# A fused retention and feed-forward kernel: the last group's seven products in another order, with PSUM tiles of their own and joined stores

## The chip, the core and the metric

The kernel runs on one core of a Trainium2 chip. A core has TensorE (PE; its weight loads are listed apart as PEld), VectorE (DVE), ScalarE (ACT), GpSimd (POOL) and SyncE (SP), each with its own queue of instructions, executed in order, and 16 DMA engines. Matmuls add into PSUM, which this kernel uses as eight banks of 512 fp32 columns on 128 partitions. The metric is device time in microseconds, the median of several runs.

## The reference

The first half is a linear recurrence per batch and head with a decay per head, the second a feed-forward layer with the activation h + sin(alpha h)^2 / alpha:

```python
for t in range(S):                                  # S = 768, B = 4, H = 8, D = 64
    state = gamma * state + k[:, :, t] (outer) v[:, :, t]
    y[:, :, t] = q[:, :, t] @ state / sqrt(D)
x = y.transpose(0, 2, 1, 3).reshape(B * S, H * D)   # 3072 tokens x 512
h = x @ w_in                                        # 512 -> 2048
s = sin(alpha * h)
g = h + s * s / (alpha + 1e-9)
out = g @ w_out                                     # 2048 -> 512, fp32
```

## The kernel before

The 3072 tokens are 24 tiles of 128, worked in ten groups (4 tiles, eight times 2, and 4). For each group the retention part fills `xT`; then 16 slots follow, one for each block of 128 of the 2048 hidden columns (in the last group). A slot is four matmuls into a PSUM tile `ph` (line 610), a sine and a square on ACT (lines 613 and 618), and one addition on DVE (line 625) that writes a block of `gT`, the transposed g. In the last group, number 9, the slots take the blocks 0, 8, 1, 9, ... 7, 15, so that slots 2m and 2m + 1 make "chunk" m: blocks m and m + 8.

Groups 8 and 9 compute `g @ w_out` with seven block products in place of eight (class `Seven`). For a pair of token tiles the hidden axis is halved (eight blocks each, index j, written `J`) and the 512 output columns are halved (`NH` = 256). Products 3 and 4 have one tile of `gT` on the left and mixed weights `w_mix` on the right; products 5 and 2 have sums of g blocks (`g_mix`, kind "s") and plain `w_out`; products 1, 7 and 6 have sums or differences of both. `g_mix` is made by three additions of line 710 for each chunk, on POOL for chunks 0 to 4 and on DVE for chunks 5, 6 and 7. A product is eight matmuls of 256 columns (line 758). `mm` chooses the accumulator by `IN`: products 5 and 2 go to the two halves of `b`, 4 and 3 to the two halves of `a`, 1 to `c`; later 7 and 6 add onto `a`.

The results leave in four steps. `hold` copies `b` out of PSUM (on ACT, line 767, in the last group). `cross` adds it to `a`, which gives the two off-diagonal output blocks (line 782). `rest` computes `c` minus the held `b` into `t_sb` (line 788). When 7 and 6 have been added, `main` adds `a` and `t_sb` for the two diagonal blocks (line 793). Each block is stored by SP (line 773). All these SBUF tiles (`b_sb`, `o_sb`, `t_sb`) rotate through five buffers, so a new one waits for the store that last read its buffer.

Group 8 is woven between the slots of group 9 (`fast_pieces`). Group 9 is the end of the program (`fast_end`): its first pair of tiles is `x`, its second `y`, and `todo` is the written order of both. For `y` (`split`), products 3 and 6 are done in two halves of 128 columns, so that the last addition and the last store are small: `main(7)`, `main(0)` and `main(1)`. `a` is then `a4` (products 4 and 7) and `a3` (3 and 6), where `a3` is one tile of two banks with a half in each, and `a4` shares the two-bank tile `a4c` with `c`. A tile is handed from writer to reader and back as a whole. PSUM tags are "mm" (four tiles of one bank, also used by the slots' `ph`) and "two" and "pa" (one tile of two banks each).

Where a slot's place carries extra work, `mixes` sets it: `mixes((9, n), f)` runs f behind slot n. The queue of each engine is what this order writes; nothing reorders it later.

Of the kernel before, what the change touches and what calls it, by code (L numbers as in the profile page):

```python
# [8 lines left out]
F32 = mybir.dt.float32  # L9
# [29 lines left out]
def kernel(  # L39
# [15 lines left out]
    nc = tc.nc  # L55
# [5 lines left out]
    d_model = H * D  # L61
# [15 lines left out]
    NG = len(sizes)  # L77
    groups = [order[sum(sizes[:g]):sum(sizes[:g + 1])] for g in range(NG)]
# [5 lines left out]
    psum = ctx.enter_context(tc.tile_pool(name="psum", bufs=1, space=bass.MemoryType.PSUM))  # L84
# [544 lines left out]
    po = {}  # L629
# [24 lines left out]
    FH, NH = FF // 2, d_model // 2  # L654
# [28 lines left out]
    def blocks(t, first, *dims):  # L683

        return bass.AP(t.tensor, t.offset + 128 * first, [t.ap[0]] + [[128 * a, n] for a, n in dims if n > 1] + [[1, 128]])

    def mix_g(g, m, n, eng):

        w = sizes[g]
        if m == 0 and w == 2:  # L690
            for k in ("s0", "s1", "d0", "d1", "x"):
                g_mix[g, k] = big.tile([128, 8 * 128], BF16, name="g_mix", tag="qkr", bufs=10)
        elif m == 0:
            for k in (2, 3):
                g_mix[g, k] = big.tile([128, 5 * 8 * 128], BF16, name="g_mix", tag=f"qk_seq{k}")
        t, h = gT[g], (2, w // 2)
        a, b = m * w, (m + FH) * w
        for op, x0, x1, (to, at), q in (
                (ALU.add, (a, (w, n), (1, w)), (b, (w, n), (1, w)), mixed_g(g, "s", m), w),
                (ALU.subtract, (a + 1, (w, n), h, (b - a - 1, 2)), (a, (w, n), h, (b - a + 1, 2)), mixed_g(g, "d", m), w),  # L700
                (ALU.add, (a, (w, n), h), (b + 1, (w, n), h), mixed_g(g, "x", m), w // 2)):
            i0, i1 = blocks(t, *x0), blocks(t, *x1)
            o = to[:, 128 * at:128 * (at + n * q)]
            if len(i0.ap) == 4:
                o = o.rearrange("p (a b i) -> p a b i", a=i0.ap[1][1], i=128)
            elif len(i0.ap) == 5:
# [3 lines left out]
            eng.tensor_tensor(o, i0, i1, op=op)  # L710

    def mixed_g(g, k, m):

        if sizes[g] == 2:
            return (g_mix[g, "x"], m) if k == "x" else (g_mix[g, f"{k}{m // 4}"], 2 * (m % 4))
        if k == "x":
            return g_mix[g, 2 + m // 4], 32 + 2 * (m % 4)
        return g_mix[g, 2 if k == "s" else 3], 4 * m

    class Seven:  # L720
# [25 lines left out]
        def mm(self, n, j, half=None):  # L746
            k = self.IN[n]
            if self.split and k == "a":
                k = "a4" if n in (4, 7) else "a3"
            t = self.bank(k)  # L750
            r = self.right(n, j)
            if k in ("a", "b"):
                o = t[:, int(n in (2, 3, 6))]
            elif k == "a3":
                o, r, k = t[:, half, 0:128], r[:, 128 * half:128 * half + 128], ("a3", half)
            else:
                o = t
            nc.tensor.matmul(o, self.left(n, j), r, start=k not in self.begun, stop=(j == FH - 1), skip_group_check=True)  # L758
            self.begun.add(k)

        def tmp(self, name):
# [6 lines left out]
            else:  # L768
                by.tensor_copy(self.bsb, self.at["b"])

        def store(self, t, s, n, lo=0, hi=None):
            hi = NH if hi is None else hi
            nc.sync.dma_start(out=out_view[:, groups[self.g][2 * self.p + t], NH * n + lo:NH * n + hi], in_=s)

        def cross(self):
            o = self.tmp("o_sb")
            if self.split:
                nc.vector.tensor_add(o[:, 0], self.at["a4"], self.bsb[:, 1])
                nc.vector.tensor_add(o[:, 1].rearrange("p (x i) -> p x i", x=2), self.at["a3"][:, :, 0:128],
                                     self.bsb[:, 0].rearrange("p (x i) -> p x i", x=2))  # L780
            else:
                nc.vector.tensor_add(o, self.at["a"], self.bsb[:, ::-1])
            self.store(1, o[:, 0], 0)
            self.store(0, o[:, 1], 1)

        def rest(self):
            self.t = self.tmp("t_sb")
# [2 lines left out]
        def main(self, which=None):  # L790
            if which is None:
                o = self.tmp("o_sb")
                nc.vector.tensor_add(o, self.at["a"], self.t)
                self.store(0, o[:, 0], 0)
                self.store(1, o[:, 1], 1)
            elif which == 7:
                self.o = self.tmp("o_sb")
                nc.vector.tensor_add(self.o[:, 0], self.at["a4"], self.t[:, 0])
                self.store(0, self.o[:, 0], 0)
            else:  # L800
                c = slice(128 * which, 128 * which + 128)
                nc.vector.tensor_add(self.o[:, 1, c], self.at["a3"][:, which, 0:128], self.t[:, 1, c])
                self.store(1, self.o[:, 1, c], 1, c.start, c.stop)

        def pieces(self, *parts):
# [293 lines left out]
    def mixes(place, fn):  # L1099
        behind_slot.setdefault(place, []).append(fn)  # L1100
# [14 lines left out]
_INS = ['q', 'k', 'v', 'moe_w_in', 'moe_w_out', 'moe_alpha']  # L1115
# [26 lines left out]
```

## Time and profile before

| | us |
|---|---|
| median of 3 runs | 208.04 |
| lowest and highest run | 207.47, 208.92 |
| the profiled execution | 206.92 |
| its span, first to last instruction | 205.1 |

The profile has one execution. Busy time by engine over the span: PE 195.5 us (95%), PEld 131.4 (64%), DVE 162.3 (79%), ACT 151.7 (74%), POOL 163.4 (80%). Rows of the timeline have the start, the duration from the first to the last end of a merged group, engine, line, operation, tiles and shape, the number of instructions, and in brackets the idle time before it and who ended it. A row that groups by shape has busy time, mean ns of one, then idle time before and its releaser. PE's matmuls overlap, so a gap in issuing is read from start times. POOL and ACT have nothing to do in the last 10 us but ACT's two copies of `b`.

### The profile page before, as it was taken

What the parts mean: (1) busy time and instruction counts of PE and PEld (TensorE: products, weight loads), DVE (VectorE), ACT (ScalarE), POOL (GpSimd) and SP (SyncE); (2) the same over time, 40 slices, a digit from 0 to 9 for tenths busy, and PEclk for the clock granted to TensorE, in tenths of its full rate; (3) what the DMA queues carried; (4) which work ended last, traced back from release to release, by engine and by line L of the source; (5) the groups of instructions that cost most, each with busy time, mean ns of one, the idle gap of its engine ahead of it and who ended that gap; (6) DMA issues with size and microseconds to landing.
All of it is one profiled execution on the core that took longest, in us unless ns stands there. A gap on an engine that the chain in (4) does not pass through costs nothing.

```text
span 205.1 us, 6031 instructions
## 1 busy us (share of the span) xinstructions
PE 195.5 (95%) x2426; PEld 131.4 (64%) x2455; DVE 162.3 (79%) x343; ACT 151.7 (74%) x312; POOL 163.4 (80%) x204
## 2 busy tenths in 40 slices
PE   7889999999999999999999999999999999999992
PEld 7545544457776676676666676766767655556982
DVE  5788599867999988878999796976977965689462
ACT  7779888557997787787687779588686779998020
POOL 8999997999979998797896979998284858994000
PEclk9999999999999999999999999999999999999998
DMA  8999999999999999999992999992714101010133
GB/s 133 153 179 193 200 202 173 167 130 141 235 128 174 96 193 184 185 136 128 212 108 54 156 94 122 116 157 56 107 51 56 54 2 51 3 51 0 54 102 102
DMA packets 103628, 24.82 MB, mean 121 GB/s; under 512 B 93440, under 2 KB 101296, under 8 KB 103600
## 3 DMA queue, kind: packets, MB, share of 16 engines
q0 software_dynamic: 80080, 13.38, 91.2%
q1 hardware_dynamic: 23520, 11.06, 26.5%
q8 instruction: 19, 0.31, 0.6%
q14 instruction: 9, 0.07, 0.1%
HBM read 27.30 MB, written 6.29 MB: 164 GB/s over the span
## 4 chain that ended last, share of the span: by engine, by line
PE 83%; DVE 6%; issue 3%; POOL 2%; DMA 2%; ACT 2%; DVEq 0%; POOLq 0%
PE ph L610 38%; PE po L634 28%; DMA qkr<-in_k_dram 2%; PE a L758 2%; PE ab L758 2%; DVE gT L625 2%; PE py L373 2%; PE b L758 1%; PE a4c L758 1%; POOL qkr L125 1%; PE pt L291 1%; POOL vr L125 1%; PE pa L388 1%; DVE g_mix L710 1%; PE py L446 1%
## 5 line engine op out<-in xcount | busy, mean ns | idle before, releaser
L610 PE MATMUL ph<-xT,w_in 128*128 128x256 bf16 (+3 forms) x653 | 98.0, 290 | 0.3
L625 DVE SCALAR_TENSOR_TENSOR gT<-s,rec_alpha,ph 128x256 bf16<-128x256 f32 (+3 forms) x164 | 79.5, 522 | 22.5 <-ACT s L618 22.0
L613 ACT ACTIVATE s<-ph,alpha_sb 128x256 f32<-128x256 f32 (+3 forms) x164 | 75.8, 505 | 26.6 <-PE ph L610 24.8
L610 PEld LDWEIGHTS <-w_in 128*128 128x128 bf16 x656 | 63.1, 98 | 29.6 <-DVE s_f L568 0.7
L634 PE MATMUL po<-w_out,gT 128*128 128x512 bf16 x264 | 70.3, 379 | 2.3 <-issue 1.9
L618 ACT ACTIVATE s<-s 128x512 f32<-128x512 f32 (+1 forms) x94 | 58.7, 625 | 2.8
L634 PEld LDWEIGHTS <-gT 128*128 128x128 bf16 x288 | 26.4, 98 | 20.9 <-DVE gT L625 0.5
L710 POOL TENSOR_TENSOR g_mix<-gT 128x512 bf16<-128x512 bf16 (+1 forms) x27 | 25.9, 992 | 7.2 <-DVE gT L625 7.2
L149 POOL DMA_DIRECT2D qk_seq<-in_q_dram x32 | 21.6, 719 | 3.1 <-DMA v_seq<-in_v_dram 1.4
L149 POOL DMA_DIRECT2D qk_seq<-in_k_dram x32 | 21.3, 705 | 2.8 <-DMA qk_seq<-in_q_dram 2.8
L149 POOL DMA_DIRECT2D v_seq<-in_v_dram x24 | 16.8, 754 | 0.0
L758 PEld LDWEIGHTS <-g_mix 128*128 128x128 bf16 x128 | 12.0, 98 | 4.6 <-issue 0.9
L681 POOL TENSOR_TENSOR w_mix<-w_out 128x1024 bf16<-128x1024 bf16 x7 | 14.9, 2150 | 0.0
L644 DVE COPY o_sb<-po 128x512 f32<-128x512 f32 x15 | 10.3, 687 | 2.0 <-PE po L634 1.6
L125 POOL DMA_DIRECT2D vr<-in_v_dram x11 | 10.3, 932 | 0.9 <-DMA w_in<-in_moe_w_in_dram 0.7
L189 POOL TENSOR_TENSOR v_seq<-v_seq,kgq 128x512 bf16<-128x512 bf16 x9 | 9.6, 1068 | 1.6 <-DMA v_seq<-in_v_dram 1.6
L407 DVE TENSOR_TENSOR aTw<-pa,maskq 128x768 bf16<-128x768 f32 x10 | 9.5, 954 | 0.2 <-PE pa L421 0.2
L495 DVE TENSOR_TENSOR xT<-py,qg 128x512 bf16<-128x512 f32 x13 | 8.9, 684 | 0.5 <-PE py L453 0.5
L864 PE MATMUL spare<-warm 128*128 128x112 bf16 (+1 forms) x52 | 7.8, 323 | 1.4 <-DVE warm L199 1.2
L391 DVE TENSOR_TENSOR aT<-pa,mask 128x1024 bf16<-128x1024 f32 x7 | 8.5, 1219 | 0.4 <-PE pa L388 0.4
L520 ACT CAST s_q<-s_f 128x256 bf16<-128x256 f32 x13 | 5.1, 395 | 3.4 <-DVE s_f L515 2.7
L125 POOL DMA_DIRECT2D qkr<-in_k_dram x7 | 6.3, 897 | 0.5 <-DMA w_in<-in_moe_w_in_dram 0.5
(141 smaller groups left out, 219.0 us busy)
## 6 DMA issues: line engine op xcount, KB each, us to landing
out_dram<-o_sb SPq DMA_DIRECT2D x18, 256.0 KB, 4.1
w_in<-in_moe_w_in_dram POOLq DMA_DIRECT2D x8, 256.0 KB, 7.9
w_out<-in_moe_w_out_dram POOLq DMA_DIRECT2D x8, 256.0 KB, 7.9
vr<-in_v_dram POOLq DMA_DIRECT2D x11, 128.0 KB, 5.3
out_dram<-o_sb SPq DMA_DIRECT2D x11, 128.0 KB, 1.8
v_seq<-in_v_dram POOLq DMA_DIRECT2D x16, 80.0 KB, 4.5
qkr<-in_q_dram POOLq DMA_DIRECT2D x7, 128.0 KB, 5.9
qkr<-in_k_dram POOLq DMA_DIRECT2D x7, 128.0 KB, 6.2
```

Source lines behind the costliest of these rows:

```text
L125: nc.gpsimd.dma_start(out=t, in_=chunk_of(src, j))
L149: nc.gpsimd.dma_start(out=o, in_=src[bt, head(b, m, e), now[0] * C:(now[-1] + 1) * C, :].rearrange("(f i) d -> i f d", i=64))
L189: eng.tensor_mul(t, t, by[:, j % NCH, :, None].to_broadcast([128, H, D]))
L610: nc.tensor.matmul(self.ph[:, m, :], w_in[:, i, f * 128:(f + 1) * 128], xT[g][:, i, self.lo:self.hi], start=(m == 0 and i == 0), stop=(i = ...
L613: nc.scalar.activation(out=self.s[:, m, :], in_=self.ph[:, m, :], func=ACTF.Sin, scale=alpha_sb[:, f:f + 1])
L618: nc.scalar.activation(out=self.s, in_=self.s, func=ACTF.Square)
L625: nc.vector.scalar_tensor_tensor(gT[self.g][:, f, self.lo:self.hi], self.s[:, m, :], rec_alpha[:, f:f + 1], self.ph[:, m, :], op0=ALU.mult ...
L634: nc.tensor.matmul(po[g, ts], gT[g][:, f, ts * C:(ts + 1) * C], w_out[:, f, :], start=(f == 0), stop=(f == FF - 1))
L644: nc.vector.tensor_copy(o_sb, po[g, ts])
L681: eng.tensor_tensor(w_mix[n, i], w_block(*a, js), w_block(*b, js), op=op)
L710: eng.tensor_tensor(o, i0, i1, op=op)
L758: nc.tensor.matmul(o, self.left(n, j), r, start=k not in self.begun, stop=(j == FH - 1), skip_group_check=True)
```

## The change

Four things change, all in the last two groups; what is computed stays.

1. `fast_end`: the first seven chunks of products 3 and 4 and the first five of 5 and 2 are done for x, then the same for y; then the last three chunks of 5 and 2, `hold`, and the eighth chunk of 3 and 4, then `cross`, for x and for y. After that x's products 1, 7, 6 with `rest` and `main` are wholly ahead of y's.
2. PSUM: x's `b` and `c` use the "pa" tag one after the other; y's `a3` becomes two tiles `a30` and `a31` of the "mm" tag, `a4` has the "two" tile alone, and y's `c` is an "mm" tile.
3. `cross` and `main` of the last group store both blocks in one transfer (`store_both`). So that one access pattern serves, the halves of `a` swap places: `main` now reads `a` reversed where `cross` read `b_sb` reversed.
4. On DVE the mix of chunk 5 moves from behind slot 12 to behind slot 14, and that of chunk 6 from behind slot 14 to behind slot 15.

```diff
         def mm(self, n, j, half=None):
...
-                k = "a4" if n in (4, 7) else "a3"
+                k = "a4" if n in (4, 7) else f"a3{half}"
             t = self.bank(k)
             r = self.right(n, j)
             if k in ("a", "b"):
-                o = t[:, int(n in (2, 3, 6))]
-            elif k == "a3":
-                o, r, k = t[:, half, 0:128], r[:, 128 * half:128 * half + 128], ("a3", half)
-            else:
-                o = t
+                t = t[:, int(n in (2, 4, 7))]
+            elif half is not None:
+                r = r[:, 128 * half:128 * half + 128]
...
+        def store_both(self, o, n):
+
+            t0, t1 = groups[self.g][2 * self.p:2 * self.p + 2]
+            if self.g < NG - 1:
+                self.store(0, o[:, 0], n)
+                self.store(1, o[:, 1], 1 - n)
+                return
+            to = bass.AP(out.tensor, out.offset + t0 * 128 * d_model + NH * n,
+                         [[d_model, 128], [(t1 - t0) * 128 * d_model + (NH if n == 0 else -NH), 2], [1, NH]])
+            nc.sync.dma_start(out=to, in_=o)
 
         def cross(self):
             o = self.tmp("o_sb")
             if self.split:
-                nc.vector.tensor_add(o[:, 0], self.at["a4"], self.bsb[:, 1])
-                nc.vector.tensor_add(o[:, 1].rearrange("p (x i) -> p x i", x=2), self.at["a3"][:, :, 0:128],
-                                     self.bsb[:, 0].rearrange("p (x i) -> p x i", x=2))
+                nc.vector.tensor_add(o[:, 1], self.at["a4"], self.bsb[:, 1])
+                for h in range(2):
+                    c = slice(128 * h, 128 * h + 128)
+                    nc.vector.tensor_add(o[:, 0, c], self.at[f"a3{h}"], self.bsb[:, 0, c])
             else:
-                nc.vector.tensor_add(o, self.at["a"], self.bsb[:, ::-1])
-            self.store(1, o[:, 0], 0)
-            self.store(0, o[:, 1], 1)
+                nc.vector.tensor_add(o, self.at["a"], self.bsb)
+            self.store_both(o, 1)
...
-                nc.vector.tensor_add(o, self.at["a"], self.t)
-                self.store(0, o[:, 0], 0)
-                self.store(1, o[:, 1], 1)
+                nc.vector.tensor_add(o, self.at["a"][:, ::-1], self.t)
+                self.store_both(o, 0)
...
     def fast_end(g):
-        J, J0, J1, J2 = range(FH), range(FH - 1), range(FH - 1, FH), range(FH - 3, FH)
-        J5 = range(FH - 3)
+        J, J0, J1 = range(FH), range(FH - 1), range(FH - 1, FH)
+        K0, K1 = range(FH - 3), range(FH - 3, FH)
 
         def near_banks(k):
-            if k == "c":
-                return psum.tile([128, NH], F32, name="c", tag="mm", bufs=4)
+            if k in ("b", "c"):
+                return psum.tile([128, 2, 512], F32, name=k, tag="pa")[:, 0].rearrange("p (x n) -> p x n", x=2)[:, slice(0, 2) if k == "b" else 0]
             return psum.tile([128, 2, NH], F32, name=k, tag="mm", bufs=4)
 
         def far_banks(k):
             if k == "b":
-                return near_banks(k)
-            if k == "a3":
-                return psum.tile([128, 2, 512], F32, name="a3", tag="pa")
-            if "a4c" not in po:
-                po["a4c"] = psum.tile([128, 2, 512], F32, name="a4c", tag="two")
-            return po["a4c"][:, int(k == "c"), 0:NH]
+                return psum.tile([128, 2, NH], F32, name=k, tag="mm", bufs=4)
+            if k == "a4":
+                return psum.tile([128, 2, 512], F32, name=k, tag="two")[:, 0, 0:NH]
+            return psum.tile([128, NH if k == "c" else 128], F32, name=k, tag="mm", bufs=4)
         x, y = Seven(g, 0, near_banks), Seven(g, 1, far_banks, True)
-        todo = x.pieces((3, J), (4, J0)) + y.pieces((3, J), (4, J0)) + x.pieces((5, J5), (2, J5)) + y.pieces((5, J5), (2, J5))
-        todo += x.pieces((4, J1)) + y.pieces((4, J1)) + x.pieces((5, J2), (2, J2), x.hold, x.cross)
-        todo += y.pieces((5, J2), (2, J2), y.hold, y.cross) + x.pieces((1, J), x.rest) + y.pieces((1, J), y.rest)
-        todo += x.pieces((7, J), (6, J), x.main)
-        todo += y.pieces((7, J), lambda: y.main(7), (6, J, 0), lambda: y.main(0), (6, J, 1), lambda: y.main(1))
+        todo = x.pieces((3, J0), (4, J0), (5, K0), (2, K0)) + y.pieces((3, J0), (4, J0), (5, K0), (2, K0))
+        todo += x.pieces((5, K1), (2, K1), x.hold, (3, J1), (4, J1), x.cross)
+        todo += y.pieces((5, K1), (2, K1), y.hold, (3, J1), (4, J1), y.cross)
+        todo += x.pieces((1, J), x.rest, (7, J), (6, J), x.main)
+        todo += y.pieces((1, J), y.rest, (7, J), lambda: y.main(7), (6, J, 0), lambda: y.main(0), (6, J, 1), lambda: y.main(1))
...
-        mixes((9, 2 * m + 1 + (m in (5, 6))), lambda m=m: mix_g(9, m, 1, nc.gpsimd if m < 5 else nc.vector))
+        mixes((9, 2 * m + 1 if m < 5 else min(15, m + 9)), lambda m=m: mix_g(9, m, 1, nc.gpsimd if m < 5 else nc.vector))
```

The change moves instructions on three engines. First DVE at the end of group 9's slots, before: the rows of line 625 are the additions of slots 12, 13, 14 and 15, those of line 710 the mixes of chunks 5 and 6 (three each), and line 793 is the last addition of group 8.

```order
L625 SCALAR_TENSOR_TENSOR gT_3495<-s_3674,rec_alpha_138,ph_3673 128x512
L710 TENSOR_TENSOR g_mix_3522<-gT_3495 128x512
L710 TENSOR_TENSOR g_mix_3523<-gT_3495 128x512
L710 TENSOR_TENSOR g_mix_3523<-gT_3495 128x256
L625 SCALAR_TENSOR_TENSOR gT_3495<-s_3689,rec_alpha_138,ph_3688 128x512
L625 SCALAR_TENSOR_TENSOR gT_3495<-s_3702,rec_alpha_138,ph_3701 128x512
L710 TENSOR_TENSOR g_mix_3522<-gT_3495 128x512
L710 TENSOR_TENSOR g_mix_3523<-gT_3495 128x512
L710 TENSOR_TENSOR g_mix_3523<-gT_3495 128x256
L793 TENSOR_TENSOR o_sb_3728<-ab_3504,t_sb_3668 128x512
L625 SCALAR_TENSOR_TENSOR gT_3495<-s_3717,rec_alpha_138,ph_3716 128x512
```

The same place now:

```order
L625 SCALAR_TENSOR_TENSOR gT_3495<-s_3674,rec_alpha_138,ph_3673 128x512
L625 SCALAR_TENSOR_TENSOR gT_3495<-s_3686,rec_alpha_138,ph_3685 128x512
L625 SCALAR_TENSOR_TENSOR gT_3495<-s_3699,rec_alpha_138,ph_3698 128x512
L710 TENSOR_TENSOR g_mix_3522<-gT_3495 128x512
L710 TENSOR_TENSOR g_mix_3523<-gT_3495 128x512
L710 TENSOR_TENSOR g_mix_3523<-gT_3495 128x256
L801 TENSOR_TENSOR o_sb_3725<-ab_3504,t_sb_3668 128x512
L625 SCALAR_TENSOR_TENSOR gT_3495<-s_3714,rec_alpha_138,ph_3713 128x512
```

The additions of slots 13 and 14 passed the mix of chunk 5, and the mix of chunk 6 went behind slot 15's addition, ahead of chunk 7's.

Second PE, at the start of the first product into `c`. Before, x's product 1 ends there and y's begins, with its wait for DVE:

```order
L758 LDWEIGHTS g_mix_3523 [waits DVE_49]
L758 MATMUL c_3826<-w_mix_2596,g_mix_3523 128x256
L758 LDWEIGHTS g_mix_3522
L758 MATMUL a4c_3769<-w_mix_2383,g_mix_3522 128x256 [waits DVE_49]
L758 LDWEIGHTS g_mix_3522
```

Now, y's eighth chunk of products 3 (two halves) and 4, then x's product 1:

```order
L756 LDWEIGHTS gT_3495
L756 MATMUL a30_3762<-w_mix_2381,gT_3495 128x128
L756 LDWEIGHTS gT_3495
L756 MATMUL a31_3770<-w_mix_2381,gT_3495 128x128
L756 LDWEIGHTS gT_3495
L756 MATMUL a4_3778<-w_mix_2333,gT_3495 128x256
L756 LDWEIGHTS g_mix_3522
L756 MATMUL c_3826<-w_mix_2383,g_mix_3522 128x256 [waits Activation_49]
```

The wait of `c` moved from y's to x's product and from DVE's additions to ACT's copy of x's `b`.

Third PE again, where y's product 6 goes from its first half of the columns to its second, before:

```order
L758 LDWEIGHTS g_mix_3523
L758 MATMUL a3_3752<-w_mix_2895,g_mix_3523 128x128
L758 LDWEIGHTS g_mix_3523
L758 MATMUL a3_3752<-w_mix_2895,g_mix_3523 128x128 [waits DVE_49]
L758 LDWEIGHTS g_mix_3523
```

and now:

```order
L756 LDWEIGHTS g_mix_3523
L756 MATMUL a30_3762<-w_mix_2895,g_mix_3523 128x128
L756 LDWEIGHTS g_mix_3523
L756 MATMUL a31_3770<-w_mix_2895,g_mix_3523 128x128 [waits DVE_49]
L756 LDWEIGHTS g_mix_3523
```

Both wait for a count of DVE's instructions. Before it was that of `main(0)`, the addition that reads the first half just written; now it is that of y's `cross`, which last read the tile `a31`.

More of the change, by code (lines that the diff above doesn't have):

```diff
@@ L752, in mm @@
             if k in ("a", "b"):
-                o = t[:, int(n in (2, 3, 6))]
-            elif k == "a3":
-                o, r, k = t[:, half, 0:128], r[:, 128 * half:128 * half + 128], ("a3", half)
-            else:
-                o = t
-            nc.tensor.matmul(o, self.left(n, j), r, start=k not in self.begun, stop=(j == FH - 1), skip_group_check=True)
+                t = t[:, int(n in (2, 4, 7))]
+            elif half is not None:
+                r = r[:, 128 * half:128 * half + 128]
+            nc.tensor.matmul(t, self.left(n, j), r, start=k not in self.begun, stop=(j == FH - 1), skip_group_check=True)
             self.begun.add(k)
@@ L769, in hold, with store @@
                 by.tensor_copy(self.bsb, self.at["b"])
-        def store(self, t, s, n, lo=0, hi=None):
-            hi = NH if hi is None else hi
+        def store(self, t, s, n, lo=0, hi=NH):
             nc.sync.dma_start(out=out_view[:, groups[self.g][2 * self.p + t], NH * n + lo:NH * n + hi], in_=s)
+        def store_both(self, o, n):
[7 more added lines that the diff above has]
+            nc.sync.dma_start(out=to, in_=o)
         def cross(self):
@@ L801, in main @@
                 c = slice(128 * which, 128 * which + 128)
-                nc.vector.tensor_add(self.o[:, 1, c], self.at["a3"][:, which, 0:128], self.t[:, 1, c])
+                nc.vector.tensor_add(self.o[:, 1, c], self.at[f"a3{which}"], self.t[:, 1, c])
                 self.store(1, self.o[:, 1, c], 1, c.start, c.stop)
```

## Prediction

> **What bounds the kernel now.** I read the page first, then the chain that ended last, then the timeline of the last 17 us engine by engine, then the waits and the output stores. TensorE (PE) is busy for 95% of the span, and the change touches only what happens after the last feed-forward slot, from about 188 us on. So the question is how much of those last 17 us is not PE work. The chain of waits there, in order of time (start us, us, what):
>
> ```profile
> 188.53 0.67 DVE gT L625
> 189.20 0.05 issue
> 189.25 1.94 PE a L758 x24
> ...
> 195.04 0.59 ACT b_sb L767
> 195.64 0.02 issue
> 195.66 0.69 DVE o_sb L782
> 196.35 0.40 DVE o_sb L778
> 196.75 0.04 issue
> 196.79 1.03 PE a4c L758 x8
> ...
> 200.93 0.30 DVE o_sb L802
> 201.24 0.04 issue
> 201.28 0.62 PE a L758 x8
> 201.90 0.02 issue
> 201.92 0.29 DVE o_sb L802
> ```
>
> Three times the chain leaves PE for VectorE (DVE) and comes back: at 189.25 PE waited for an addition that makes gT, at 196.79 for the addition of line 778, at 201.28 for the addition of line 802. To price these I need the pace at which PE issues when nothing holds it. The timeline of PE has the groups ahead of each wait, and the groups by shape have the length of one matmul:
>
> ```profile
> 187.98 0.93 PE L758 MATMUL a<-w_mix,gT 128*128 128x256 bf16 x7
> 195.50 1.04 PE L758 MATMUL c<-w_mix,g_mix 128*128 128x256 bf16 x8
> 200.28 0.61 PE L758 MATMUL a<-w_mix,g_mix 128*128 128x128 bf16 x8
> ...
> L758 PE MATMUL c<-w_mix,g_mix 128*128 128x256 bf16 x8 | 1.0, 272 | 0.0
> L758 PE MATMUL a<-w_mix,g_mix 128*128 128x128 bf16 x16 | 1.2, 219 | 0.4 <-DVE o_sb L802 0.4
> ```
>
> Eight matmuls of 256 columns in 1.04 with the last one 0.27 long are (1.04 - 0.27)/7 = 0.110 us apart; eight of 128 columns are (0.61 - 0.22)/7 = 0.056 apart. So the eighth `a` was due at 187.98 + 7 x 0.110 = 188.75 and came at 189.25: **0.50** lost. The first `a4c` was due at 195.50 + 8 x 0.110 = 196.38 and came at 196.79: **0.41**. The second half of `a3` was due at 200.28 + 8 x 0.056 = 200.73 and came at 201.28: **0.55**. Together 1.46 us. Everything else from 187.98 on is PE issuing back to back.
>
> **The change part by part.** The amount of PE work stays: the same 128 matmuls (40 + 56 of 256 columns, 32 of 128) are issued in another order. Where PE starts also stays, because ScalarE (ACT) paces the slots before it and none of its instructions moves. These are ACT, GpSimd (POOL) and DVE near that place, and the busy time in the stretch 184 to 188 us (PE, PEld, DVE, ACT, POOL, clock, DMA):
>
> ```profile
> 184.00:188.00 4.00, 4.00 (x28) 2.44 (x26) 3.66 (x7) 3.90 (x8) 3.05 (x4) 1.00 0.07 25
> ...
> 187.27 0.63 ACT L618 ACTIVATE s<-s 128x512 f32<-128x512 f32 x1
> 188.51 0.63 ACT L618 ACTIVATE s<-s 128x512 f32<-128x512 f32 x1
> ...
> 184.15 2.90 POOL L710 TENSOR_TENSOR g_mix<-gT 128x512 bf16<-128x512 bf16 x3
> ...
> 186.11 1.76 DVE L710 TENSOR_TENSOR g_mix<-gT 128x512 bf16<-128x512 bf16 x3
> 187.80 1.39 DVE L625 SCALAR_TENSOR_TENSOR gT<-s,rec_alpha,ph 128x512 bf16<-128x512 f32 x2
> 189.11 0.95 DVE L710 TENSOR_TENSOR g_mix<-gT 128x512 bf16<-128x512 bf16 x3
> 189.99 0.68 DVE L793 TENSOR_TENSOR o_sb<-ab,t_sb 128x512 f32<-128x512 f32 x1
> 190.59 0.73 DVE L625 SCALAR_TENSOR_TENSOR gT<-s,rec_alpha,ph 128x512 bf16<-128x512 f32 x1
> ```
>
> ACT is busy 3.90 of 4.00 us and ends the squares of slots 14 and 15 at 187.90 and 189.14.
>
> *Eighth chunks last, mixes moved on DVE.* The wait at 189.25 is for chunk 7, which slot 14's addition writes; its square ended at 187.90, but DVE was in the mix of chunk 5, which took 1.76 because POOL mixed until 187.05 (the next mix took 0.95). Now that mix stands behind slot 14's addition. My DVE times: slot 14's addition 187.92 to 188.65, mix 5 to 189.60, the last output addition of group 8 to 190.28, slot 15's addition to 191.01, mixes 6 and 7 to 192.92. PE's times at 0.110 and 0.056: x's 14 of products 3 and 4 to 189.52, its 10 of products 5 and 2 to 190.62, y's 14 half-width to 191.40 and 7 wide to 192.17, its 10 to 193.27. Nothing waits: the accumulator `a4` needs group 8's addition (190.28, reached at 191.40), y's `b` needs slot 15's buffer (191.01, reached 192.17), the last chunks of products 5 and 2 need mix 7 (192.92, reached 193.27), chunk 7 of products 3 and 4 is reached only at 193.9. Saved: 0.50. The tightest cover is mix 7's, 0.35 us; its first instruction alone is what products 5 and 2 read, so the true cover is larger.
>
> *Own accumulators.* y's product 1 (`c`) no longer lies in one tile with `a4`, so its 0.41 goes. In its place x's `c` takes over the tile of x's `b` and so waits for the ACT copy of line 767, and x's product 7 waits for x's cross addition. ACT and DVE take:
>
> ```profile
> L767 ACT COPY b_sb<-b 128x512 f32<-128x512 f32 x2 | 1.2, 585 | 6.0 <-PE b L758 5.9
> L782 DVE TENSOR_TENSOR o_sb<-a,b_sb 128x512 f32<-128x512 f32 x1 | 0.7, 692 | 3.3 <-ACT b_sb L767 3.3
> L793 DVE TENSOR_TENSOR o_sb<-a,t_sb 128x512 f32<-128x512 f32 x1 | 0.7, 692 | 1.1 <-PE a L758 1.1
> L802 DVE TENSOR_TENSOR o_sb<-a,t_sb 128x128 f32<-128x128 f32 x2 | 0.6, 292 | 0.7 <-PE a L758 0.7
> L778 DVE TENSOR_TENSOR o_sb<-a4c,b_sb 128x256 f32<-128x256 f32 x1 | 0.4, 425 | 0.0
> L779 DVE TENSOR_TENSOR o_sb<-a,b_sb 128x256 f32<-128x256 f32 x1 | 0.4, 415 | 0.0
> ```
>
> x's last `b` is issued by 193.93 and ends 0.16 later; the copy runs 194.11 to 194.70. PE meanwhile issues two matmuls of x, y's six and three of y, to 195.04: the copy is covered by 0.34 us. x's cross addition ends at 195.41, product 7 is reached at 195.92: cover 0.51. The new waits cost 0.
>
> *The two halves of product 6 apart.* `a3` becomes two tiles, so the second half no longer waits for the reading of the first: 0.55 saved. No row shows PE writing one half while DVE reads the other, so the price lies between 0 and the whole 0.55; the nearest row is PE issuing 128-column matmuls at 0.056 from 200.28 while DVE read `a4c` from 200.49, undisturbed, and I take 0. The Trainium skill, PSUM — Partial Sum Buffer, section on bank collisions, has engines kept apart by bank (and quadrant of partitions); the halves already lay in two banks, so by it the old wait came from the tile alone and all 0.55 goes; a hold in the chip itself would leave 0.91 of the 1.46. The undisturbed row agrees with the page.
> y's cross now adds the halves in two instructions: 2 x 0.292 - 0.415 = 0.17 more on DVE. They end near 196.6, and x's last addition is due only at 197.8: covered, 0. If DVE were late, x's product outputs would be, not PE.
>
> *Stores.* From x's cross on SyncE issues 6 transfers where it issued 9. Its issues and their landings, and two stretches (engines as above, then the clock, the DMA engines' share and GB/s):
>
> ```profile
> L773 SPq DMA_DIRECT2D out_dram<-o_sb x13: 332/399/424, 182.6 to 202.2; - x13
> DMA to landing us min/median/max: 1.7/1.8/1.8
> ...
> DMA to landing us min/median/max: 2.0/3.1/6.7
> ...
> 194.00:196.00 2.00, 2.00 (x21) 1.80 (x19) 0.34 (x1) 0.89 (x2) 0.00 (x0) 1.00 0.00 0
> 201.50:202.00 0.50, 0.38 (x7) 0.21 (x4) 0.08 (x1) 0.00 (x0) 0.00 (x0) 1.00 0.81 273
> ```
>
> The first landing row is of these stores, the second of line 647's, 256 KB each in the middle of the kernel. An issue costs SyncE 0.33 to 0.42. Fewer issues earlier save nothing, since the last store (64 KB, split as before) still follows the last addition; the price of the joined form is unknown, between the 1.8 of 128 KB and the 6.7 of a 256 KB store. I take 1.8 plus 128 KB more at the 273 GB/s of the last row, 0.5: 2.3 us. Who needs it: y's `t_sb` reuses the buffer of x's cross and waits for its store (issued about 195.45, landed 197.75, needed 198.72 when y's `c` is done), and x's joined store waits for the same landing on SyncE, with y's last three stores queued behind it. Cover 0.97: cost 0. Group 8's swap of which operand is read backwards is 0 too: line 782 with a reversed operand takes 0.692, line 793 without one 0.692 as well.
>
> **Sum.** -0.50 - 0.41 - 0.55 = -1.46. PE's last matmul moves from 201.90 to 200.44 (the paces added up from 187.98 give 200.50), the last addition from 202.21 to 200.75; what follows it (2.89 us to the end of the span) stays. The profiled execution took 206.92 for a span of 205.1; it would become 205.46. That execution lies 1.12 under the median of the runs, 208.04, so the forecast on the median is 208.04 - 1.46 = **206.6 us**, 0.7% faster. About 1% is what a measurement of this kernel can tell from no change.
>
> **The rivals.**
> *A new wait takes the old ones' place.* If x's ACT copy or its cross addition comes over 0.3 to 0.5 us later than I put it, PE stands before `c` or `a` again. The old hand-overs cost 0.41 and 0.55; two such back leave 1.46 - 0.96 = 0.50: 207.5. For it: the covers of 0.34 to 0.51 are small. Against it: in the old chain the copy began 0.02 after its releaser and took its 0.59.
> *The end is not PE's.* If the stores' own stream set the end, an earlier PE would bring nothing: 208.0. For it: in 201.5 to 202.0 the DMA engines are 81% busy. Against it: the last store landed in the shortest time of all, 1.7, and now the same bytes are spread over a longer stretch.
> *The joined store lands late (slower).* It has 198.72 - 195.45 = 3.27 us. From 3.27 + 1.46 = 4.7 on the kernel is slower than before; at the 6.7 of the longest 256 KB store it is 6.7 - 3.27 = 3.43 later than my forecast: 210.0. Against it: those stores ran beside loads, and here the DMA share is 0.00 in 194 to 196; their median of 3.1 would still just do. [...]
>
> **How the numbers follow.** Forecast 0.66, a new wait 0.17, the end not PE's 0.11, the late store 0.06. Runs of the kernel before lie within 1.45 of each other, half of which, 0.73, I allow on the forecast: 205.85 to 207.3. The range reaches up to the new wait's 207.5 with 0.3 of that allowance, 207.8, and down to 205.5 by half of it more, since the median shown may itself stand high beside its profile. It leaves out the last two rivals, 0.17. Faster by over 1% means under 205.96, a quarter of the forecast's case: 0.17. Slower by over 1% means above 210.1, half of the late store and a little noise: 0.04. Within 1%: 0.79.
>
> **What would show it.** Right: no PE gap of 0.3 us or more between 188 and the last matmul, which comes about 12.4 us after the first `a`; mix 5 at 0.95; PE's waits for the additions of the old lines 778 and 802 gone; y's `t_sb` not waiting for a DMA. Wrong: PE waiting for ACT before x's `c`, for DVE before x's product 7 or before the last chunks of products 5 and 2, joined stores over 3.3 us to landing, or a later first `a`.

## The result, and the profile after

| us | before | after |
|---|---|---|
| median of 20 runs each | 207.75 | 206.38 |
| ratio to before, 95% interval | | 0.9937, 0.9913 to 0.9962 |
| the profiled execution, its span | 206.92, 205.1 | 207.02, 205.2 |
| first matmul into x's `a` | 187.98 | 189.66 |
| end of the last DVE addition | 202.21 | 202.41 |
| the stretch between the two | 14.23 | 12.75 |
| the tail, from there to the end of the span | 2.89 | 2.79 |

The kernel is 0.63% faster, with the interval 1.31 us, 0.79 to 1.81: inside the forecast's range, and within 1%, as forecast. One of the 20 executions of before took 407.21 us; without it their median is 207.68. The one profiled execution of the kernel after does not show it in its span, which is 0.1 longer. It reached the first matmul into x's `a` 1.68 us later than the execution of before, and up to there the two programs do the same work but for one moved mix; the distance stood already long before, while data was still loaded (SP issued one and the same store of line 647 at 74.17 before and at 75.99 after). So the two are compared from that matmul on: 1.48 us less in the stretch and 0.10 less in the tail. Spans are printed to a tenth of a microsecond here, so a tail is good to 0.05; in the trace the two spans are 205.125 and 205.227, and the tails 2.91 and 2.81.

The chain of waits after, in order of time (start us, us, what):

```profile
189.38 0.44 PE ab L756 x4
189.82 1.53 PE a L756 x14
191.35 1.09 PE b L756 x10
192.44 1.55 PE a L756 x21
193.99 1.75 PE b L756 x16
...
196.82 0.87 PE c L756 x8
197.70 1.75 PE a L756 x16
199.44 0.87 PE c L756 x8
200.32 1.78 PE a L756 x24
202.10 0.02 issue
202.12 0.29 DVE o_sb L809
```

In the chain of before DVE stood three times between two stretches of PE. Now the chain stays on PE from the last slots to the last matmul, and only the last addition follows. The busy time by engine over the stretch says the same. First of the kernel after, then of the kernel before (PE, PEld, DVE, ACT, POOL, clock, DMA share, GB/s):

```profile
189.60:202.20 12.60, 12.48 (x131) 11.21 (x128) 8.91 (x22) 2.35 (x4) 0.00 (x0) 1.00 0.24 85
```

```profile
187.90:202.30 14.40, 13.00 (x131) 11.19 (x128) 8.78 (x19) 2.38 (x5) 0.00 (x0) 1.00 0.23 77
```

PE is idle for 0.12 of 12.60 us, where it was idle for 1.40 of 14.40. The view of PE's waits in this part of the program has three rows before, and none after:

```profile
PE a L758 <- DVE o_sb L802: 0.4, 1, 0.4
PE a L758 <- DVE gT L625: 0.3, 1, 0.3
PE a4c L758 <- DVE o_sb L778: 0.3, 1, 0.3
```

How near the new hand-overs are is read from the timeline after:

```profile
192.40 1.83 DVE L710 TENSOR_TENSOR g_mix<-gT 128x512 bf16<-128x512 bf16 x6
193.82 1.91 PE L756 MATMUL b<-w_out,g_mix 128*128 128x256 bf16 x16
...
195.77 0.58 ACT L765 COPY b_sb<-b 128x512 f32<-128x512 f32 x1 [4.95 <-PE b L756]
...
196.38 0.69 DVE L791 TENSOR_TENSOR o_sb<-a,b_sb 128x512 f32<-128x512 f32 x1 [2.15 <-ACT b_sb L765]
...
196.66 1.04 PE L756 MATMUL c<-w_mix,g_mix 128*128 128x256 bf16 x8
...
197.53 1.91 PE L756 MATMUL a<-w_mix,g_mix 128*128 128x256 bf16 x16
```

x's copy of `b` ends at 196.35 and x's `c` takes over the tile at 196.66: 0.31 to spare. x's cross addition ends at 197.07 and product 7 starts at 197.53: 0.46. The mixes of chunks 6 and 7 end at 194.23; the last chunks of products 5 and 2 are the last six of the group at 193.82, reached ten matmuls of 0.110 later, at 194.92: 0.69.

### The profile page after: what moved, and what is told of

It reads as the page before. It is cut to its first block, busy times and chain, and to the rows that moved or that the text cites. A ratio compares the mean times of both kernels' runs of the same rounds, so it can differ in the third digit from the quotient of the medians.

```text
span 205.2 us, 6029 instructions
## 1 busy us (share of the span) xinstructions
PE 195.2 (95%) x2426; PEld 131.4 (64%) x2455; DVE 161.5 (79%) x344; ACT 151.8 (74%) x312; POOL 163.2 (80%) x204
## 4 chain that ended last, share of the span: by engine, by line
PE 83%; DMA 7%; POOL 4%; issue 2%; DVE 2%; ACT 1%; POOLq 0%
PE ph L610 37%; PE po L634 28%; DMA qkT<-qkr 4%; PE a L756 3%; DMA qkr<-in_q_dram 3%; PE ab L756 3%; POOL qkr L125 2%; PE b L756 2%; PE py L373 1%; POOL vr L125 1%; PE c L756 1%; PE pt L291 1%; PE pa L388 1%; PE py L437 1%; POOL w_in L161 1%
## 5 line engine op out<-in xcount | busy, mean ns | idle before, releaser
L165 POOL DMA_DIRECT2D w_out<-in_moe_w_out_dram x8 | 5.8, 727 | 1.2 <-DMA w_in<-in_moe_w_in_dram 0.8
```

## The experiments

The theory: three stalls of PE were the whole difference, each is removed by one part of the change, and the stores bring nothing. The rivals: a part does nothing here, or removes another part's stall too; the new hand-overs are nearly late; the end is set by something other than PE. Since the time up to the first `a` differs from one execution to the next, each kernel is judged by the stretch and the tail as defined above:

| | first `a` | last addition's end | stretch | span | tail |
|---|---|---|---|---|---|
| before | 187.98 | 202.21 | 14.23 | 205.1 | 2.89 |
| after | 189.66 | 202.41 | 12.75 | 205.2 | 2.79 |
| before, with the mixes moved | 195.78 | 209.50 | 13.72 | 212.4 | 2.90 |
| after, mixes in the old places | 189.92 | 202.68 | 12.76 | 205.5 | 2.82 |
| after, `c` beside `a4` | 188.37 | 202.07 | 13.70 | 204.9 | 2.83 |
| after, `a3` one tile | 188.48 | 201.78 | 13.30 | 204.4 | 2.62 |
| after, stores apart | 188.17 | 200.93 | 12.76 | 204.0 | 3.07 |
| after, x's copy twice | 188.17 | 201.28 | 13.11 | 204.1 | 2.82 |
| after, old order of products 1, 7, 6 | 196.25 | 209.00 | 12.75 | 211.9 | 2.90 |
| after, five matmuls fewer | 188.42 | 200.63 | 12.21 | 203.5 | 2.87 |

**The mixes alone.** The kernel before, with only the fourth part of the change.

```diff
-        mixes((9, 2 * m + 1 + (m in (5, 6))), lambda m=m: mix_g(9, m, 1, nc.gpsimd if m < 5 else nc.vector))
+        mixes((9, 2 * m + 1 if m < 5 else min(15, m + 9)), lambda m=m: mix_g(9, m, 1, nc.gpsimd if m < 5 else nc.vector))
```

> The kernel before with only the mixes of chunks 5 and 6 moved on DVE (part 4 of the change). I measure the end stretch: from the first matmul into x's a to the end of the last addition; it is 14.23 us in the kernel before and 12.75 in the changed one. My theory, that the first of the three stalls is slot 14's addition standing behind the 1.76 us mix: that addition now ends near 0.7 us after the first a, the stall of 0.50 goes or shrinks under 0.1, the other two (0.41 and 0.55) stay, the stretch is 13.75. Rival, that only the later place of chunk 7 in PE's order removes it: the stretch stays at 14.2.

The stretch is 13.72, 0.51 under that of before. Of the three waits of PE two are left:

```profile
PE a L758 <- DVE o_sb L802: 0.4, 1, 0.4
PE a4c L758 <- DVE o_sb L778: 0.3, 1, 0.3
```

So the wait for chunk 7 goes by the moved mix alone. Its time as a whole, 214.18, has nothing to do with the end: 7 us were lost from 104 us on (see the last section).

**The mixes back.** The kernel after, with that line as it was before (the diff above the other way round).

> The changed kernel with the mixes of chunks 5 and 6 where they were. Theory: PE reaches chunk 7 of products 3 and 4 only about 6 us after its first a, and mix 7 keeps over 0.3 us of cover, so nothing waits: stretch 12.75. Rival, that moving the mixes carries the first stall's 0.50: 13.25.

The stretch is 12.76, no longer. The mix of chunk 5 took 1.76 us again, between slot 12's and slot 14's additions, and no one waits for it, since chunk 7 is now first read at 195.84, 4.7 us behind slot 14's addition. So the 0.50 is removed by the late eighth chunk or by the moved mix, by either alone; with the new order the fourth part of the change has no share in the time.

**`c` beside `a4`.** The kernel after, with y's `c` and `a4` in one tile of two banks as before.

```diff
-            if k == "a4":
-                return psum.tile([128, 2, 512], F32, name=k, tag="two")[:, 0, 0:NH]
-            return psum.tile([128, NH if k == "c" else 128], F32, name=k, tag="mm", bufs=4)
+            if k in ("a4", "c"):
+                if "a4c" not in po:
+                    po["a4c"] = psum.tile([128, 2, 512], F32, name="a4c", tag="two")
+                return po["a4c"][:, int(k == "c"), 0:NH]
+            return psum.tile([128, 128], F32, name=k, tag="mm", bufs=4)
```

> The changed kernel with y's c again in the second bank of the tile that holds y's a4. Theory: y's product 7 now comes right behind product 1, so with one tile it must wait until t_sb has read c (c's last matmul ends 0.16 after product 7 could start, the subtraction takes 0.69): a PE stall of 0.9, stretch 13.65. Rival, that the old stall of 0.41 came from the order of the products alone: 12.75; or it comes back as it was: 13.15.

The stretch is 13.70, and PE's row before y's product 7 has the reason:

```profile
197.99 1.04 PE L756 MATMUL a4c<-w_mix,g_mix 128*128 128x256 bf16 x8
199.81 1.03 PE L756 MATMUL a4c<-w_mix,g_mix 128*128 128x256 bf16 x8 [0.78 <-DVE t_sb L796]
```

Product 1 ends, DVE reads `c` into `t_sb`, and only then product 7 may write `a4` in the same tile. In the order of before x's products 7 and 6 stood between them. So the shared tile costs 0.95 in the new order, more than the 0.41 that it cost in the old one: the order with x wholly ahead can be had only with the tile of its own.

**`a3` as one tile.** The kernel after, with the two halves in two banks of one tile, and `a4` in a one-bank tile.

```diff
-            if k == "a4":
-                return psum.tile([128, 2, 512], F32, name=k, tag="two")[:, 0, 0:NH]
-            return psum.tile([128, NH if k == "c" else 128], F32, name=k, tag="mm", bufs=4)
+            if k[:2] == "a3":
+                if "a3" not in po:
+                    po["a3"] = psum.tile([128, 2, 512], F32, name="a3", tag="two")
+                return po["a3"][:, int(k[2]), 0:128]
+            return psum.tile([128, NH], F32, name=k, tag="mm", bufs=4)
```

> The changed kernel with y's a30 and a31 again as the two banks of one tile (a4 in a tile of its own instead). Theory: the second half of product 6 waits for the addition that reads the first, 0.55 comes back, stretch 13.30. Rival, that the new order hides it: 12.75.

The stretch is 13.30: the whole 0.55 is back, at the old place.

```profile
200.85 0.61 PE L756 MATMUL a<-w_mix,g_mix 128*128 128x128 bf16 x8 [0.38 <-DVE o_sb L809]
```

The banks of the halves are two in both kernels; only the tile differs. With two tiles PE writes one half while DVE reads the other, and nothing is held: the 24 matmuls from 200.16 in the kernel after follow each other at the pace of before. The Trainium skill, PSUM — Partial Sum Buffer, section on bank collisions, lets two engines work on different banks at once; the runs agree, with 0.55 against 0.

**Stores apart.** The kernel after, with nine stores again in place of six.

```diff
-            if self.g < NG - 1:
+            if self.g < NG:
```

> The changed kernel with the joined stores of the last group as two stores each again. Theory: the stores are off the path, stretch 12.75 and the tail from the end of the last addition to the end of the span 2.8 as now, within 0.1. Rival, that fewer stores shorten the tail (it is 2.79 now, 2.89 in the kernel before): the tail is 2.9 or more.

The stretch is the same, 12.76, and the tail is 3.07, the rival's side: the stores were not worth nothing. What differs is looked at in the runs on the tail below.

**x's copy twice.** The kernel after, with ACT's copy of x's `b` made two times, one after the other.

```diff
-                nc.scalar.copy(self.bsb, self.at["b"])
+                for _ in range(2 - self.p):
+                    nc.scalar.copy(self.bsb, self.at["b"])
```

> The changed kernel with x's b copied twice by ACT, so that the copy that c waits for ends 0.6 us later. It measures the cover of the new wait, 0.31 by the trace of the changed kernel. Theory: PE stands 0.6 - 0.3 = 0.3 before x's c, x's product 7 keeps waiting for nothing, stretch 13.05. Rival, a new wait that already sets the pace: the whole 0.6, stretch 13.35. If the copy were of no account: 12.75.

The stretch grew by 0.36, to 13.11, where the copy had grown by 0.59:

```profile
195.53 1.03 PE L756 MATMUL c<-w_mix,g_mix 128*128 128x256 bf16 x8 [0.20 <-ACT b_sb L766]
```

So the copy has some 0.23 to spare up to the point at which PE's issue is really late (0.59 - 0.36), a little less than the 0.31 between its end and `c`, of which the hand-over takes part. The tightest of the new waits is this one.

**The old order of the last products.** The kernel after, with products 1, 7 and 6 in the order of before, on the new tiles.

```diff
-        todo += x.pieces((1, J), x.rest, (7, J), (6, J), x.main)
-        todo += y.pieces((1, J), y.rest, (7, J), lambda: y.main(7), (6, J, 0), lambda: y.main(0), (6, J, 1), lambda: y.main(1))
+        todo += x.pieces((1, J), x.rest) + y.pieces((1, J), y.rest) + x.pieces((7, J), (6, J), x.main)
+        todo += y.pieces((7, J), lambda: y.main(7), (6, J, 0), lambda: y.main(0), (6, J, 1), lambda: y.main(1))
```

> The changed kernel with x's product 1 and y's product 1 in a row again, then x's 7 and 6, then y's 7 and 6 (the first pair no longer wholly ahead), with the new tiles. Theory: with c in a tile of its own the order of the products brings nothing to PE, stretch 12.75; x's last store of 256 KB leaves 0.9 us later and meets the last three, so the tail may grow from 2.79 to 2.9. Rival, that having the first pair ahead carries the 0.41: 13.15.

The stretch is 12.75. Once `c` has its own tile, having x wholly ahead brings nothing. (This execution also lost 7 us from 104 us on, see the last section.)

**Five matmuls fewer.** The kernel after, without the first five matmuls of x's product 2.

```diff
-        todo = x.pieces((3, J0), (4, J0), (5, K0), (2, K0)) + y.pieces((3, J0), (4, J0), (5, K0), (2, K0))
+        todo = x.pieces((3, J0), (4, J0), (5, K0)) + y.pieces((3, J0), (4, J0), (5, K0), (2, K0))
```

> The changed kernel without the first five matmuls of x's product 2, whose part of the sum is left out. Theory, that PE's issuing sets the end: 5 x 0.11 = 0.55 less, stretch 12.2, unless mix 7, which had about 0.7 of cover, is met: down to 12.2 all the same. Rival, that DVE or the stores set the end: 12.75 or a tail longer by 0.5.

The stretch is 12.21, 0.54 less: five times 0.110. What PE issues still comes out at the end in full, so the end is PE's, and the stores do not set it.

**The tail.** The tail has two pieces: from the end of the last addition to SP's issue of the last store, and from there to the end of the span. SP's stores at the end, their issue and landing, by line; the last number before the semicolon is when the last one was issued. Before, after, and with the stores apart:

```profile
L773 SPq DMA_DIRECT2D out_dram<-o_sb x9: 332/399/424, 196.4 to 202.2; - x9
```

```profile
L770 SPq DMA_DIRECT2D out_dram<-o_sb x3: 345/384/393, 201.7 to 202.6; - x3
...
DMA to landing us min/median/max: 1.6/1.7/1.8
```

```profile
L770 SPq DMA_DIRECT2D out_dram<-o_sb x9: 332/382/443, 195.6 to 201.1; - x9
...
DMA to landing us min/median/max: 1.7/1.7/1.8
```

By the timeline the last issue was at 202.24 before, 0.03 after its addition; at 202.60 after, 0.19 behind it; at 201.10 with the stores apart, 0.17 behind it. So the kernel after lost 0.16 here: its last two additions start 0.44 apart (201.68 and 202.12), where before the stall of 0.55 had set them 0.99 apart, and an issue of 0.35 to 0.39, with the wait ahead of it, does not fit in between any more. With the stall back (`a3` as one tile) the last store is issued at 201.81, 0.03 behind its addition again, and the tail is 2.62, the shortest of the first eight runs. From the last issue to the end it is 2.86 before and 2.90 with nine stores, 2.60 after with six, though the last store lands in 1.6 to 1.7 in all of them. Two runs went after the two pieces.

One store on ACT's queue: the small store of `main(0)` is issued by ACT, which has nothing else to do there.

```diff
-        def store(self, t, s, n, lo=0, hi=NH):
-            nc.sync.dma_start(out=out_view[:, groups[self.g][2 * self.p + t], NH * n + lo:NH * n + hi], in_=s)
+        def store(self, t, s, n, lo=0, hi=NH, by=nc.sync):
+            by.dma_start(out=out_view[:, groups[self.g][2 * self.p + t], NH * n + lo:NH * n + hi], in_=s)
...
-                self.store(1, self.o[:, 1, c], 1, c.start, c.stop)
+                self.store(1, self.o[:, 1, c], 1, c.start, c.stop, nc.sync if which else nc.scalar)
```

> The kernel after, with one store, that of the last token tile's first half of its main block, issued from ACT's queue instead of SP's, so that SP issues only one store in the last 0.6 us. In the kernel after, SP was still issuing the store before until 202.50, and issued the last one at 202.60, 0.19 us after the addition's end at 202.41. Theory (SP's issuing delays the last store, and the tail carries the delay): the stretch from the first matmul into x's a to the last addition's end stays 12.75 us, the last store is issued 0.03 to 0.05 us after the addition, and the tail falls from 2.79 to about 2.63 us, so the whole is 0.15 us below the kernel after, 1.46 us below before. Rival (what follows the last landing takes the gain back, or ACT's queue is later at it): the tail stays at 2.75 us or more.

The first `a` is at 188.43, the last addition ends at 201.18, the span is 203.8: a stretch of 12.75 and a tail of 2.62, and SP issued its last store 0.03 after the addition, in the timeline:

```profile
200.77 0.37 ACTq L770 DMA_DIRECT2D out_dram<-o_sb  x1
...
201.21 0.34 SPq L770 DMA_DIRECT2D out_dram<-o_sb  x1
```

Its median is 205.51, and the ratio to before 0.9888 (0.9856 to 0.9921). This is 0.87 under the median of the kernel after, far more than the 0.17 of the tail, so both were timed side by side on one chip, as they are. The kernel after:

> The kernel after as it stands, timed beside the version with one store on ACT's queue, on one chip. The single profiles give that version 0.17 us less behind the last addition (2.62 against 2.79 us) and the same stretch before it, 12.75 us. Theory (the store's queue is all that differs, the rest of the distance between the two medians, 206.38 and 205.51 us, is spread from the loading phase): the two medians here lie 0.1 to 0.5 us apart. Rival (moving that store also changes what comes before): they lie 0.8 us or more apart, as they did.

And the one with a store on ACT's queue:

> The version with one store on ACT's queue, beside the kernel after on the same chip. Theory: its median is 0.1 to 0.5 us under that kernel's, and the tail of its profile is 2.6 us again, with a stretch of 12.75 us. Rival: 0.8 us or more under it; or no difference at all, with a tail of 2.75 us or more.

The medians are 205.93 and 205.66, 0.27 apart; the stretches 12.76 and 12.75; the tails 2.78 (204.4 - 201.62) and 2.65 (203.9 - 201.25). By the unrounded spans of the traces the tail is shorter by 0.17 in the first pair of executions and by 0.18 in the second, so this part is repeatable. Their ratios to before, 0.9902 (0.9867 to 0.9936) and 0.9909 (0.9878 to 0.9940), don't tell the two apart, so by timing alone it is not settled that this version beats the kernel after.

Fourteen stores: the stores of the last group's two joined forms in halves, one of them whole.

```diff
+            if True:
+                w = NH // 2
+                for t, m in ((0, n), (1, 1 - n)):
+                    s = o[:, t]
+                    if n == 0 and t == 0:
+                        self.store(t, s, m)
+                        continue
+                    for h in range(2):
+                        self.store(t, s[:, w * h:w * h + w], m, w * h, w * h + w)
+                return
```

> The kernel after, with the stores of the last group's first two blocks cut into halves instead of joined, one whole: 14 stores in all. With nine stores the tail was 3.07 us, with six 2.79 us. The stretch from the first matmul into x's a to the last addition's end should stay 12.75 us. Theory (at the end SP looks at the stores' semaphores in a fixed order, and what counts is how many it has still to look at behind the last store's own: with 14 stores the last store is on the same semaphore as with six): the tail is 2.7 to 2.85 us. Rival (the number of stores counts): the tail is 3.07 us or more.

The first `a` is at 188.96, the last addition ends at 201.72, the span is 205.1: the stretch is 12.76 as expected, but the tail is 3.38: by that number the rival's. It is so because the first piece of it grew: SP was issuing without a break and came to the last store only at 202.55, 0.83 behind its addition.

```profile
L770 SPq DMA_DIRECT2D out_dram<-o_sb x14: 332/410/452, 196.4 to 202.5; - x14
```

```profile
202.55 0.40 SPq L770 DMA_DIRECT2D out_dram<-o_sb  x1
```

The second piece, from the last issue to the end, is 2.55, as short as with six stores (2.60 in both runs of the kernel after, 2.59 and 2.62 with one store on ACT, 2.69 at most in the other runs) and not the 2.86 to 2.90 of the three runs with nine. So what counts in it is not how many stores there are.

The records of SP's queue show what does. The program gives its transfers eight semaphores in turn, and at its end SP checks these eight one after the other in a fixed order. The last of six stores has the last semaphore in that order, and so has the last of fourteen, eight more; the last of nine has the third. SP's checks from the landing of the last store on, first of the kernel before, then of the kernel after:

```profile
L1137 SPq EVENT_SEMAPHORE  x6: 27/28/28, 203.9 to 204.2; - x6
```

```profile
L1142 SPq EVENT_SEMAPHORE  x1: 28/28/28, 204.3 to 204.3; - x1
```

The five checks more are 0.06 apart, 0.30 together. By the same records the time from the landing of the last store to the end of the span is 1.23 in each of the three runs with nine stores and 0.91 to 0.93 in the eleven with six or fourteen. So the mechanism that the run was made for is shown, and the number of stores matters only in where it leaves the last one in that order.

## Why the prediction was right, and where it was off

*What bounds the kernel.* Right. PE's issue sets the end after (the chain), five matmuls fewer shorten it by their own 0.54, and the rivals that had it elsewhere are out. One of the signs named for being wrong did show, a later first `a` (189.66 against 187.98). But that delay was there at the store of line 647, at 75.99 against 74.17, ahead of all that the change moves, so it says nothing about the change.

*Eighth chunks last, mixes moved: -0.50.* Right in size; the step names two edits for one stall, and either does it alone (13.72 from the mixes without the order, 12.76 from the order without the mixes). The mix of chunk 5 takes 0.95 as foreseen. The cover of mix 7 was put at 0.35 and is 0.69.

*Own accumulators: -0.41.* Right. The covers of the new hand-overs, put at 0.34 and 0.51, are 0.31 and 0.46, and the doubled copy shows that the first is real. That is also why the rival "a new wait takes the old ones' place" stayed away: it needed 0.3 us of delay and none came. What the step did not say is that the two edits it treats together depend on each other: with the shared tile the new order would have cost 0.95.

*The halves of product 6 apart: -0.55.* Right, with all of it taken away by the tile and nothing kept by the chip.

*The sum.* -1.46 was forecast for the stretch and -1.48 came; the last matmul ends 12.44 us after the first `a`, where about 12.4 was forecast. On the medians the whole gain is 1.37, and 1.31 with 0.79 to 1.81 by the ratio. The second timing of the same kernel, in the run beside the ACT version, has a ratio of 0.9902, about 2.0 us. The 1.58 of the traces lies between the two. The forecast of 206.6 started from 208.04, the median of three runs, which stands 0.29 above that of twenty; that is more than all that parts 206.6 from 206.38.

*The stores: 0, and the tail stays at 2.89.* Mis-sized, by about 0.1 in sum. The landing was taken at 2.3 and came at 2.1, with SP's wait for it inside its cover:

```profile
L781 SPq DMA_DIRECT2D out_dram<-o_sb x3: 372/383/383, 197.1 to 200.2; - x3
...
DMA to landing us min/median/max: 2.1/2.1/2.1
```

But the step "fewer issues earlier save nothing, since the last store still follows the last addition" left out both ends of the tail. Behind the last issue 0.26 is saved (2.86 to 2.60), because the last of six stores happens to have the semaphore that SP checks last (0.3, of which a landing 0.07 longer took a part). And the removed stall brings the last two stores so close together that SP is 0.16 late with the last one. Together -0.10, and -1.58 with the stretch, inside the interval. That the two leave so little of each other is luck: neither was foreseen. The rival "the joined store lands late" needed 3.27 us and got 2.1.

## What to carry to other kernels

Stalls read as gaps in issuing, on an engine that is shown to set the end, add up to the change in that stretch to within a few hundredths of a microsecond, as long as the cover of each new wait is worked out too. A hand-over of a whole tile can be a stall that the banks do not ask for: give readers and writers of different halves different tiles, and check this again when the order around them changes. When a stall ahead of the last stores goes, look at the queue that issues them: 0.35 to 0.4 us for each issue is enough to delay the last one, and an idle engine's queue can take one of them. What SP still has to check behind the last landing counts too, 0.06 us for each check here.

## What the runs showed of the hardware beside this

Two of the executions, that with the mixes alone and that with the old order of products, reached the end stretch some 7 us later than the others, by a place that no edit touched. It is one addition on DVE of two SBUF operands, which took 5.87 and 5.78 us there. DVE and POOL in the first of the two, from the timeline:

```profile
98.86 4.93 POOL L149 DMA_DIRECT2D qk_seq<-in_k_dram  x8
103.61 5.87 DVE L189 TENSOR_TENSOR v_seq<-v_seq,kgq 128x512 bf16<-128x512 bf16 x1
103.69 3.16 POOL L189 TENSOR_TENSOR v_seq<-v_seq,kgq 128x512 bf16<-128x512 bf16 x3
106.70 2.22 POOL L681 TENSOR_TENSOR w_mix<-w_out 128x1024 bf16<-128x1024 bf16 x1
...
110.31 1.87 PE L634 MATMUL po<-w_out,gT 128*128 128x512 bf16 x4 [4.44 <-DVE gT L625]
```

And in the kernel after:

```profile
102.61 4.28 POOL L149 DMA_DIRECT2D qk_seq<-in_k_dram  x7 [0.51 <-DMA qk_seq<-in_q_dram]
...
105.09 0.68 DVE L189 TENSOR_TENSOR v_seq<-v_seq,kgq 128x512 bf16<-128x512 bf16 x1
...
107.88 3.05 POOL L189 TENSOR_TENSOR v_seq<-v_seq,kgq 128x512 bf16<-128x512 bf16 x3
```

Where the addition ran beside POOL's issuing of loads, it took 0.68. Where it started within 0.1 us of POOL's three additions, it ended (109.48) only behind all of POOL's chain (108.92), and PE stood still for 4.44. In the kernel before it took 1.43. The Trainium skill, SBUF — State Buffer, section "Who interferes with whom", has the two engines share a port pair as an exclusive lock in such a case, and the later one blocked until the other is done. The rows agree that one engine stood until the other was done, but by their start times DVE was the earlier one, by 0.08, and it lost to four instructions of POOL in a row, not to one. It was not tried apart.

The addition is 5.19 of the 7.6 us that this execution is behind the one with x's copy twice, which reached the addition at the same time. The rest arose right after it, when PE had stood still: the granted clock was 0.57 in 108 to 112 us and 0.58 in 112 to 116, where it was 1.00 in the execution with the copy twice. In the execution with the old order of products it was 0.75 and 0.82 there. How much of the rest is the clock's was not taken apart. When the addition meets POOL's chain seems to depend on when loads land, and so a change elsewhere can set it off or not; between single executions it is larger than all that this change does.
